# A planner that counts GpSimd's transfers on the common line of transfers, a release time for the accumulations of w_in, and batch 3 masked by TensorE

## The chip, the cores and the metric

The kernel runs on one core of a Trainium2 chip. Its time is the device time of one launch in microseconds (us); the time before is the median of three runs. The profile is of one further execution. The engines are named as in the profile: PE (TensorE, matrix products), DVE (VectorE), ACT (ScalarE), POOL (GpSimd) and SP (SyncE). SP does nothing but issue transfers; POOL issues those that add to what is already in SBUF.

## The reference

The program is an attention with two branches and, on its output, an MLP whose non-linearity is a rational function. Cut to what matters:

```
# q, k, v: 8 batches x 8 heads x 576 positions x 64
out_d     = softmax(mean4(q) @ mean4(k).T / 8) @ mean4(v)       # 144 pooled positions
out_up    = repeat(out_d, 4)
out_local = softmax(where(|i-j| < 4, q @ k.T / 8, -1e9)) @ v
x = (out_up + out_local)                                        # as 4608 tokens x 512
h = x @ w_in                                                    # 512 x 2048
P = a0 + a1 h + a2 h^2 + a3 h^3
Q = 1 + |b0||h| + |b1| h^2
out = (P / (Q + 1e-6)) @ w_out                                  # 2048 x 512
```

All inputs are float64 on the host's side, and w_in and w_out reach the chip as 64-bit words.

## The kernel before

**Blocks and steps.** The tokens are cut into nine blocks of 512: the first 512 tokens of each batch, and a last block of the eight leftovers of 64. A block takes 16 steps, one for each chunk of 128 of the 2048 hidden columns; 144 steps in all. Step n has a *first product* h(n) in PE (line 907 for the first sixteen steps, as plain fp32 with eight records in the profile each; from step 16 on line 919, with both factors split into a high and a low part and three of the four partial products), then the *rational function* (`middle`), and two steps later (`LAG = 2`) a *second product* into the output's banks (`o_part`, line 985, 12 matmuls of split parts). `middle` is six operations of ACT (all recorded at line 932: Abs, Square and two Identity from PSUM, which is what the names `m<-psum` and `gb<-psum` show; then Ln, `gb<-m`, and Exp, `m<-gb`) and seven of DVE (lines 947, 952 and 956, then 959, which writes the high part of g, 962, 967, and 968, which writes its low part).

**Weights.** They come in sixteen loads of 1 MB (`weights`; SP, line 356), each of two chunks of w_in or w_out, into six spots named sx0, sx1 and sl0 to sl3. sl2 and sl3 lie over attention tiles of batch 0. A load has to be turned from 64-bit words into fp32: ACT scales the upper words in place (line 363), DVE puts the parts together (366 and 369). w_out is then cast to its high part by ACT (399) and DVE takes the low part (402). w_in is used whole in the first sixteen steps, and split only after its use (`parts`): ACT writes the negative of the rounded word into the low part `wl` (line 424), POOL adds the exact word `wb` to it by an accumulating transfer (`accumulate`, line 411), and ACT then rounds the word in place to the high part `wh` (line 426).

**Attention.** `attend(b)` handles a batch in two halves of two pairs of heads. The pooled branch needs sums over four neighbours: `load_pooled` loads one of four slices by SP (line 466) and adds the other three by accumulating transfers of POOL (line 470), for two tiles pq (pooled q and k) and one tile vpc (pooled v). SP also loads qk (454) and vw (458) for the local branch. Batch 0 has its own code at the program's start. For the local scores there are two ways. In the batches that `PEMASK` lists, `scores` puts the mask into PSUM by four matmuls (line 491) ahead of the products, and `softmax_local` takes the maximum by DVE (line 534) and the exponentials by ACT (line 573) straight from PSUM. In the other batches `Half.scores` multiplies (line 700), DVE adds the mask on the way from PSUM to SBUF (line 713), and maximum (724) and exponentials (735) read SBUF.

**What sets the order.** No order is written by hand. Each operation is a task, added with its engine, a cost in us, what it reads and writes, and for some a due time (`Plan.add`). `Plan.run` first carries due times back from each task to its predecessors: the latest start of a task is that of its successor less its own cost and a lag (a fixed one by engine, or the task's own `lag`, 6.5 for an accumulation of w_in). It then plays the program forward on five engines: on each, of the tasks whose inputs are there, the one with the earliest latest start goes next (`HOLD` lets an engine wait a moment for a more urgent one). The instructions are then issued in the order of the planned starts. The plan sets only this order; on the chip an instruction waits for what it reads and for what stands ahead of it in its engine's queue. Two numbers set most due times: `due_h(n)`, the due time of step n's first product, is `H0` plus 6.11 for each of the first sixteen steps and 6.25 for each later one; a second product is due `O_LAG` steps behind that. Loads of the start have due times of their own (`LOADS`), which don't depend on H0; the due times of batch 0's attention do.

**Warm-up matmuls.** In planned idle time of PE at the start, `warm` (line 1124) puts dummy matmuls, up to the first task that is due at `due_h(0)`.

Of the kernel before, what the change touches and what calls it, by code (L numbers as in the profile page):

```python
# [14 lines left out]
ALU = mybir.AluOpType  # L15
# [9 lines left out]
POOL = 4  # L25
# [42 lines left out]


class Task:  # L70
    __slots__ = ("engine", "dur", "fn", "due", "preds", "succs", "late", "start", "end", "n", "lag", "uses")


class Plan:
# [8 lines left out]
        self.writer = {}  # L83
        self.readers = {}

    def add(self, engine, dur, fn, reads=(), writes=(), due=None, lag=None):
        t = Task()
        t.engine, t.dur, t.fn, t.due, t.n = engine, dur, fn, due, len(self.tasks)
        t.lag, t.preds, t.succs, t.late, t.start = lag, {}, [], 1e9, None
        rk = set().union(*(r.keys for r in reads)) if reads else set()  # L90
        wk = set().union(*(w.keys for w in writes)) if writes else set()
        t.uses = {k[1]: k in wk for k in rk | wk if k[0] == "P"}
        for k in rk | wk:
            w = self.writer.get(k)
            if w is not None:
                t.preds[w] = True
        for k in wk:
            for r in self.readers.get(k, ()):
                t.preds.setdefault(r, False)
            self.writer[k] = t  # L100
            self.readers[k] = []
        for k in rk - wk:
            self.readers[k].append(t) if k in self.readers else self.readers.__setitem__(k, [t])
        t.preds.pop(t, None)
        for p in t.preds:
            p.succs.append(t)
        self.tasks.append(t)
        return t
# [8 lines left out]
    def run(self):  # L117
# [8 lines left out]
        free = dict.fromkeys(self.LAG, 0.0)  # L126

        def release(t):
            at = 0.0
            for p in t.preds:  # L130
                at = max(at, p.end + self.gap(p, t))
            heapq.heappush(waiting[t.engine], (at, t.n, t))
# [5 lines left out]
        while len(done) < len(self.tasks):  # L138
            best = None
            for e in self.LAG:  # L140
                if open_[e]:
                    at = free[e]
# [26 lines left out]
                t = o[2]  # L169
            t.start, t.end = at, at + t.dur  # L170
            free[e] = t.end
            done.append(t)
            for s in t.succs:
                left[s] -= 1
# [9 lines left out]
def attention_moe(  # L184
# [162 lines left out]
    def weights(w, f, spot, due=None):  # L347
# [30 lines left out]
        if added:  # L378
            hi, lo = high2[w][f // 2], low2[w][f // 2]
            if f >= CAST:  # L380
                add(
                    "POOL", 1.0, lambda: nc.gpsimd.dma_start(out=flat2(hi), in_=flat2(word).bitcast(F32)),
                    (room,), (hi,), lag=CLAG,
                )
            else:
                add("ACT", 0.88, lambda: nc.scalar.copy(out=hi.ap, in_=word.ap.bitcast(F32)), (room,), (hi,))
# [21 lines left out]
    def accumulate(lo, word, room, due=None):  # L408
        add(
            "POOL", 1.0,  # L410
            lambda: nc.gpsimd.dma_start(out=flat2(lo), in_=flat2(word).bitcast(F32), accum_op=ALU.add),
            (room, lo), (lo,), due=due, lag=ALAG,
        )

    def parts(w, f, due=None):
# [44 lines left out]
    def load_pooled(cs):  # L460
# [4 lines left out]
        for dst, cost, src in loads:  # L465
            add("SP", cost, lambda d=dst, x=src[0]: nc.sync.dma_start(out=d.ap, in_=x), (), (dst,))
            for x in src[1:]:
                add(
                    "POOL", 1.0,
                    lambda d=dst, x=x: nc.gpsimd.dma_start(out=d.ap, in_=x, accum_op=ALU.add),  # L470
                    (dst,), (dst,), lag=4.0,
                )

    def pool_qk(c):
# [459 lines left out]
    def middle(n):  # L934
# [16 lines left out]
        )  # L951
        add("DVE", 0.61, lambda: v.tensor_tensor(out=ta.ap, in0=ta.ap, in1=tq.ap, op=ALU.mult), (ta, tq), (ta,))  # L952
        if UN[0] <= n < UN[1]:
            add("POOL", 0.95, lambda: nc.gpsimd.dma_start(out=ta.ap, in_=u.ap, accum_op=ALU.add), (ta, u), (ta,), lag=ULAG)
        else:
            add("DVE", 0.61, lambda: v.tensor_tensor(out=ta.ap, in0=ta.ap, in1=u.ap, op=ALU.add), (ta, u), (ta,))  # L956
        act(0.63, log, tb, tb.ap, AF.Ln, bias=cone)
# [82 lines left out]
    for r, x in enumerate(vf):  # L1040
# [1 line left out]
        add(  # L1042
            "POOL", 1.0,
            lambda r=r, x=x: nc.gpsimd.dma_start(out=x.ap, in_=vp[0, 2 + r], accum_op=ALU.add),
            (x,), (x,), lag=7.0,
        )
    early = LOADS[3]
    for (w, f, spot), due in zip(chunks[: len(early)], early):
# [109 lines left out]
NAT = 16  # L1158
HFIRST = (7, 5)
LAG = 2  # L1160
O_LAG = 2.11
H0 = 25.89
H_FIRST = 6.11
H_STEP = 6.25
SPLIT_EARLY = 9.53
# [8 lines left out]
DEFER = 1  # L1174
CAST = 99
CLAG = 6.0
NEG = 1
MINUS = (0, 1, 2, 3)
ADDED = (99, 99)
PEMASK = (1, 2)  # L1180


_OUTS = [((NT, DM), "float32")]
# [63 lines left out]
```

## Time and profile before

| | |
|---|---|
| median of 3 runs | 971.71 us (971.13 to 972.02) |
| the profiled execution | 968.8 us |
| its span in the trace | 966.9 us |
| granted PE clock, mean | 0.993 |
| PE busy | 943.1 us, 98% |
| DVE busy | 843.7 us, 87% |
| ACT busy | 813.4 us, 84% |
| POOL busy | 120.8 us, 12% |
| transfers by SP and hardware queues (q1) | 63.52 MB, 19.6% of 16 engines' span |
| transfers issued by POOL (q0) | 24.50 MB, 17.4% |

"Busy" counts the time in which an engine has an instruction under way, and an operation that waits inside for data may count as busy. The granted clock is 1.00 where PE may run at full rate. In a row of the timeline the first number is the start in us from the span's begin, the second the length, and a bracket behind it the idle time ahead of it on its engine with what ended that. Buffer numbers are left out there: sl stands for sl0 to sl3, wh for all high parts. A DMA row's time is that of its issue; when the data has landed is a separate number.

### The profile page before, as it was taken

How to read it: one execution, taken by the hardware profiler on the slowest of the kernel's cores; microseconds unless marked ns; L12 is line 12 of the kernel's file. 1: busy time of each engine (PE TensorE's matmuls, PEld its weight loads, DVE VectorE, ACT ScalarE, POOL GpSimd, SP SyncE). 2: the span in 40 equal slices, each digit the busy share in tenths (PEclk: the TensorE clock that was granted, in tenths of full speed). 3: DMA queues.
4: the chain of work that ended last, by engine and by line, in shares of the span. 5: the costliest groups of instructions: out<-in, count | busy, mean ns of one | idle time of the engine just before them, and what ended most of it. 6: DMA issues, size and time to landing. Idle time of an engine off the chain costs nothing.

```text
span 966.9 us, 19321 instructions
## 1 busy us (share of the span) xinstructions
PE 943.1 (98%) x7192; PEld 740.8 (77%) x7192; DVE 843.7 (87%) x1434; ACT 813.4 (84%) x1992; POOL 120.8 (12%) x144
## 2 busy tenths in 40 slices
PE   7879999999999999999999999999999999999996
PEld 5546657887888788787887787878878888888885
DVE  7779999898888989898889898898979899988885
ACT  3789999999789897979798979988797977778774
POOL 1212112021202020212111110212021000000000
PEclk9989999999999999999999999999999999999998
DMA  9995386344433433333333433334332010001001
GB/s 296 314 333 136 113 224 116 117 78 106 81 102 57 106 59 112 74 82 76 91 91 70 93 68 107 57 102 70 98 69 58 1 44 1 1 1 45 1 0 44
DMA packets 44318, 89.26 MB, mean 92 GB/s; under 512 B 4992, under 2 KB 25856, under 8 KB 44224
## 3 DMA queue, kind: packets, MB, share of 16 engines
q1 hardware_dynamic: 25344, 63.52, 19.6%
q0 software_dynamic: 18880, 24.50, 17.4%
q8 instruction: 57, 0.93, 0.4%
q14 instruction: 37, 0.30, 0.1%
HBM read 74.37 MB, written 9.44 MB: 87 GB/s over the span
## 4 chain that ended last, share of the span: by engine, by line
PE 59%; DVE 20%; ACT 14%; issue 4%; DMA 2%; DVEq 0%; POOL 0%; SPq 0%; ACTq 0%; POOLq 0%
PE psum L985 27%; PE psum L919 24%; ACT el L735 4%; ACT m L932 3%; DVE g L959 3%; DVE m L962 2%; DVE m L967 2%; PE psum L907 2%; ACT epc L599 2%; DVE m L956 2%; DVE g L968 2%; DMA sl<-in_w_in_dram 2%; ACT epc L616 2%; DVE m L952 1%; DVE m L947 1%
## 5 line engine op out<-in xcount | busy, mean ns | idle before, releaser
L985 PE MATMUL psum<-wh,g 128*128 128x512 f32 x1152 | 393.1, 402 | 7.8 <-DVE g L959 5.9
L932 ACT ACTIVATE m<-psum,cf 128x512 f32<-128x512 f32 x288 | 214.1, 748 | 60.1 <-PE psum L919 52.1
L985 PEld LDWEIGHTS psum<-wh,g 128*128 128x128 f32 x1152 | 214.4, 188 | 62.2 <-DVE g L959 9.6
L919 PE MATMUL psum<-xs,wh 128*128 128x512 f32 x1024 | 260.6, 394 | 0.0
L985 PE MATMUL psum<-wl,g 128*128 128x512 f32 x576 | 225.4, 392 | 0.0
L919 PEld LDWEIGHTS psum<-xs,wh 128*128 128x128 f32 x1024 | 189.5, 188 | 41.4 <-issue 1.2
L959 DVE TENSOR_TENSOR g<-m,m 128x512 fp32r<-128x512 f32 x144 | 99.4, 690 | 78.5 <-ACT m L932 73.0
L919 PE MATMUL psum<-xs,wl 128*128 128x512 f32 x512 | 137.5, 390 | 0.0
L985 PEld LDWEIGHTS psum<-wl,g 128*128 128x128 f32 x576 | 109.0, 189 | 23.2 <-issue 1.7
L932 ACT ACTIVATE gb<-psum,cf 128x512 f32<-128x512 f32 x144 | 115.7, 804 | 12.8 <-PE psum L985 12.8
L932 ACT ACTIVATE gb<-m,cf 128x512 f32<-128x512 f32 x144 | 107.4, 746 | 19.2 <-DVE m L947 14.8
L470 POOL DMA_DIRECT2D pq<-in_qkp_dram x84 | 73.7, 922 | 366.0 <-DMA pq<-in_qkp_dram 275.5
L919 PEld LDWEIGHTS psum<-xs,wl 128*128 128x128 f32 x512 | 95.9, 188 | 20.4 <-issue 0.2
L932 ACT ACTIVATE m<-gb 128x512 f32<-128x512 f32 x144 | 93.5, 649 | 20.7 <-DVE m L952 19.2
L947 DVE SCALAR_TENSOR_TENSOR m<-m,cf,m 128x512 f32<-128x512 f32 x144 | 107.3, 745 | 3.3 <-ACT m L932 3.2
L956 DVE TENSOR_TENSOR m<-m,gb 128x512 f32<-128x512 f32 x144 | 98.7, 685 | 6.5
L962 DVE SCALAR_TENSOR_TENSOR m<-m,g 128x512 f32<-128x512 f32 x144 | 99.2, 689 | 3.4
L968 DVE TENSOR_TENSOR g<-m,m 128x512 fp32r<-128x512 f32 x144 | 98.6, 685 | 3.3
L967 DVE TENSOR_TENSOR m<-m,m 128x512 f32<-128x512 f32 x144 | 99.0, 687 | 2.2
L952 DVE TENSOR_TENSOR m<-m,m 128x512 f32<-128x512 f32 x144 | 98.4, 683 | 0.0
L932 ACT ACTIVATE m<-psum 128x512 f32<-128x512 f32 x144 | 88.4, 614 | 0.0
L735 ACT ACTIVATE el<-el,nm 128x64 f32<-128x64 f32 x200 | 66.7, 336 | 1.4 <-DVE nm L729 0.7
(78 smaller groups left out, 920.3 us busy)
## 6 DMA issues: line engine op xcount, KB each, us to landing
qk<-in_qk_dram SPq DMA_DIRECT2D x32, 590.0 KB, 3.9
pq<-in_qkp_dram POOLq DMA_DIRECT2D x84, 144.0 KB, 3.3
vw<-in_vw_dram SPq DMA_DIRECT2D x32, 320.0 KB, 4.0
out_dram<-xf SPq DMA_DIRECT2D x32, 256.0 KB, 2.4
vpc<-in_vp_dram POOLq DMA_DIRECT2D x42, 168.0 KB, 3.5
sx<-in_w_in_dram SPq DMA_DIRECT2D x5, 1024.0 KB, 13.6
sl<-in_w_out_dram SPq DMA_DIRECT2D x4, 1024.0 KB, 16.7
sx<-in_w_out_dram SPq DMA_DIRECT2D x4, 1024.0 KB, 8.1
```

The source lines that it names most:

```text
L470: lambda d=dst, x=x: nc.gpsimd.dma_start(out=d.ap, in_=x, accum_op=ALU.add),
L735: nc.scalar.activation(out=e[:, n], in_=e[:, n], func=AF.Exp, bias=nm[:, n : n + 1], scale=scale, accum_out=sm[:, n : n + 1],)
L919: nc.tensor.matmul(ph.ap[:, f * t : (f + 1) * t], lhsT=(high, low)[j][0][fc].ap[:, c, :], rhs=blk.x[i].ap[:, c, :] if blk.b is not None el ...
L932: add("ACT", cost, lambda: nc.scalar.activation(out=out_.ap, in_=in_, func=func, **kw), (room_in, cf, *more), (out_,))
L947: lambda: v.scalar_tensor_tensor(out=tb.ap, in0=tq.ap, scalar=b1, in1=tb.ap, op0=ALU.mult, op1=ALU.add),
L952: add("DVE", 0.61, lambda: v.tensor_tensor(out=ta.ap, in0=ta.ap, in1=tq.ap, op=ALU.mult), (ta, tq), (ta,))
L956: add("DVE", 0.61, lambda: v.tensor_tensor(out=ta.ap, in0=ta.ap, in1=u.ap, op=ALU.add), (ta, u), (ta,))
L959: add("DVE", 0.61, lambda: v.tensor_tensor(out=gh.ap, in0=ta.ap, in1=tq.ap, op=ALU.mult), (ta, tq), (gh,))
L962: lambda: v.scalar_tensor_tensor(out=tb.ap, in0=tb.ap, scalar=CONE, in1=gh.ap.bitcast(F32), op0=ALU.add, op1=ALU.mult),
L967: add("DVE", 0.61, lambda: v.tensor_tensor(out=tb.ap, in0=ta.ap, in1=tb.ap, op=ALU.subtract), (ta, tb), (tb,))
L968: add("DVE", 0.61, lambda: v.tensor_tensor(out=gl.ap, in0=tb.ap, in1=tq.ap, op=ALU.mult), (tb, tq), (gl,))
L985: nc.tensor.matmul(ob[sub].ap, lhsT=g[i].ap[:, f0 : f0 + P], rhs=flat((high, low)[j][1][fc].ap), start=(fc == 0 and m == 0), stop=(fc == N ...
```

## The change

It has three parts, all in the planner's input; no operation of steps, weights or softmax is written differently.

1. *Transfers of POOL count on SP's line.* A task may carry a `load`. When such a task is planned, SP's line is busy from then on for that long (3.0 us for an accumulation of w_in, 0.8 for one of pq or vpc, 1.5 for one of vf), and the task's own lag becomes the time until that line is free again plus 2.2 us.
2. *The accumulations of w_in have a release time.* A task may carry an `after`, before which the plan does not start it; for an accumulation it is its due time plus 12.08 us. As the due time is 2 us ahead of the first split product of that chunk (step 16 and on), the plan's release lies behind step 16's first product.
3. *Constants.* `O_LAG` goes from 2.11 to 2.09, `H0` from 25.89 to 14.21, so that all due times of steps are 11.68 us earlier in the plan, and `PEMASK` takes in batch 3.

```diff
-    def add(self, engine, dur, fn, reads=(), writes=(), due=None, lag=None):
+    def add(self, engine, dur, fn, reads=(), writes=(), due=None, lag=None, load=0.0, after=0.0):
...
+        t.load, t.after = load, after
...
         def release(t):
-            at = 0.0
+            at = t.after
             for p in t.preds:
                 at = max(at, p.end + self.gap(p, t))
...
             t.start, t.end = at, at + t.dur
             free[e] = t.end
+            if t.load:
+                free["SP"] = max(free["SP"], t.end) + t.load
+                t.lag = free["SP"] - t.end + 2.2
...
     def accumulate(lo, word, room, due=None):
             lambda: nc.gpsimd.dma_start(out=flat2(lo), in_=flat2(word).bitcast(F32), accum_op=ALU.add),
-            (room, lo), (lo,), due=due, lag=ALAG,
+            (room, lo), (lo,), due=due, lag=ALAG, load=3.0, after=0.0 if due is None else due - DEFERRED,
...
     def load_pooled(cs):
-                    (dst,), (dst,), lag=4.0,
+                    (dst,), (dst,), lag=4.0, load=0.8,
...
-O_LAG = 2.11
-H0 = 25.89
+O_LAG = 2.09
+H0 = 14.21
+DEFERRED = -12.08
-PEMASK = (1, 2)
+PEMASK = (1, 2, 3)
```

Two further places that get a `load` (a cast by POOL and a sum inside `middle`) are switched off by other constants. In the changed kernel the lines of the body stand four further down: 363 is 367, 411 is 415, 932 is 936, 985 is 989.

The order of the instructions changes at the program's start, on ACT, POOL and SP, and there are 24 warm-up matmuls fewer on PE (32 instead of 56). ACT around step 0, whose first operations of the rational function are `m2_134<-psum` and `m4_136<-psum`; `sx0` is a spot of weights, `wl0_4` the low part of a chunk of w_in, `up` a part of batch 0's attention output. Before:

```order
L839 ACTIVATE up0_160<-psum 64x144
L839 ACTIVATE up1_161<-psum 64x144
L363 ACTIVATE sx0_189<-sx0_189 128x1024
L424 ACTIVATE wl0_4_58<-wb0_4_85 128x1024
L932 ACTIVATE m2_134<-psum,cf_150 128x512
L932 ACTIVATE m4_136<-psum 128x512
```

and now:

```order
L843 ACTIVATE up0_160<-psum 64x144
L843 ACTIVATE up1_161<-psum 64x144
L936 ACTIVATE m2_134<-psum,cf_150 128x512
L936 ACTIVATE m4_136<-psum 128x512
L936 ACTIVATE m0_132<-psum,cf_150 128x512
```

The scaling of sx0 and the copy into wl0_4 have left the place ahead of step 0; the scaling now stands behind step 3. Further on, ACT around step 1, whose last two operations of the six are Ln (`gb3_145<-m3_135`) and Exp (`m5_137<-gb3_145`). Before:

```order
L932 ACTIVATE m3_135<-psum,cf_150 128x512
L932 ACTIVATE m5_137<-psum 128x512
L363 ACTIVATE sl2_193<-sl2_193 128x1024
L363 ACTIVATE sl3_194<-sl3_194 128x1024
L932 ACTIVATE m0_132<-psum,cf_150 128x512
L932 ACTIVATE gb3_145<-m3_135,cf_150 128x512
L573 ACTIVATE el0_167,sm0_156<-psum,nm0_152 128x64 x5
```

and now:

```order
L936 ACTIVATE m3_135<-psum,cf_150 128x512
L936 ACTIVATE m5_137<-psum 128x512
L367 ACTIVATE sl2_193<-sl2_193 128x1024
L936 ACTIVATE m0_132<-psum,cf_150 128x512
L936 ACTIVATE gb3_145<-m3_135,cf_150 128x512
L936 ACTIVATE m2_134<-psum,cf_150 128x512
L577 ACTIVATE el0_167,sm0_156<-psum,nm0_152 128x64 x5
L936 ACTIVATE m5_137<-gb3_145 128x512
```

One scaling instead of two stands there now; that of sl3 has moved behind step 2's exponential.

The transfers that POOL issues, from batch 1's sums on (`wl0_0<-wb0_0` is the first accumulation of w_in). Before:

```order
L470 DMA pq0_165<-in_qkp_dram 128x288
L470 DMA pq1_170<-in_qkp_dram 128x288
L411 DMA wl0_0_56<-wb0_0_81 128x1024
L470 DMA pq0_165<-in_qkp_dram 128x288
L470 DMA pq1_170<-in_qkp_dram 128x288
L470 DMA vpc_174<-in_vp_dram 112x384
L411 DMA wl0_2_57<-wb0_2_83 128x1024
```

and now, the second half of batch 1 with what follows:

```order
L474 DMA pq0_165<-in_qkp_dram 128x288
L474 DMA pq1_170<-in_qkp_dram 128x288
L474 DMA vpc_174<-in_vp_dram 112x384 x3
L415 DMA wl0_0_56<-wb0_0_81 128x1024
L474 DMA pq0_165<-in_qkp_dram 128x288
L474 DMA pq1_170<-in_qkp_dram 128x288
```

All sums of both halves of batch 1 now come ahead of the first accumulation, where three accumulations stood between those of its first half; the second accumulation stands two rounds of batch 2's pq sums further on.

SP's order moves with them: sl2's load, once issued behind vpc, sx0, vw0 and vw1, now comes directly behind qk1 and ahead of those four; sl3's comes right behind vpc's. On ACT the two casts of line 426 for wh0_0 and wh0_2 now stand behind step 13's exponential. In batch 3 four pairs change from the rows of lines 713, 724 and 735 to those of 491, 534 and 573, and in batches 4 to 7 a handful of rows around their tenth and eleventh steps change places.

More of the change, by code (lines that the diff above doesn't have):

```diff
@@ L70 @@
 class Task:
-    __slots__ = ("engine", "dur", "fn", "due", "preds", "succs", "late", "start", "end", "n", "lag", "uses")
+    __slots__ = ("engine", "dur", "fn", "due", "preds", "succs", "late", "start", "end", "n", "lag", "uses", "load", "after")
 class Plan:
@@ L382, in weights @@
                     "POOL", 1.0, lambda: nc.gpsimd.dma_start(out=flat2(hi), in_=flat2(word).bitcast(F32)),
-                    (room,), (hi,), lag=CLAG,
+                    (room,), (hi,), lag=CLAG, load=3.0,
                 )
@@ L953, in middle @@
         if UN[0] <= n < UN[1]:
-            add("POOL", 0.95, lambda: nc.gpsimd.dma_start(out=ta.ap, in_=u.ap, accum_op=ALU.add), (ta, u), (ta,), lag=ULAG)
+            add("POOL", 0.95, lambda: nc.gpsimd.dma_start(out=ta.ap, in_=u.ap, accum_op=ALU.add), (ta, u), (ta,), lag=ULAG, load=1.5)
         else:
@@ L1044, in attention_moe @@
             lambda r=r, x=x: nc.gpsimd.dma_start(out=x.ap, in_=vp[0, 2 + r], accum_op=ALU.add),
-            (x,), (x,), lag=7.0,
+            (x,), (x,), lag=7.0, load=1.5,
         )
```

## The prediction

> **What bounds the kernel now.** I read first the busy times by stretch, then the chain that ended last where TensorE (PE) is idle, then the rows of ScalarE (ACT) and PE around that place. The page's first line and the stretches (columns: length, then PE, weight loads, VectorE (DVE), ACT and GpSimd (POOL) busy, granted PE clock, DMA share, GB/s):
>
> ```profile
> span 966.9 us, 19321 instructions
> 40.00:63.30 23.30, 16.65 (x93) 8.34 (x83) 13.94 (x25) 14.89 (x36) 7.02 (x8) 0.93 1.08 299
> 63.30:67.00 3.70, 3.70 (x49) 2.71 (x50) 3.20 (x6) 3.70 (x10) 0.00 (x0) 0.54 1.05 351
> 67.00:130.00 63.00, 63.00 (x434) 39.22 (x434) 61.61 (x104) 61.83 (x158) 9.87 (x11) 1.00 0.58 164
> 130.00:205.00 75.00, 74.51 (x511) 55.49 (x510) 70.74 (x122) 73.50 (x179) 14.91 (x17) 1.00 0.57 132
> 205.00:780.00 575.00, 573.36 (x4736) 462.61 (x4735) 503.26 (x890) 503.71 (x1346) 80.80 (x94) 1.00 0.36 79
> ```
>
> From 67 us on PE never rests for more than a few tenths; there only PE work counts. From 67 to 205 ACT and DVE are nearly as full (1.2 and 1.5 us, 1.4 and 4.3 us idle). Time is lost before that: in 40 to 63.3 PE is idle for 6.6 us while the DMA engines are full, and the clock drops. The chain there (start, us, what):
>
> ```profile
> 40.30 0.38 SPq L356
> 40.78 17.30 DMA sl<-in_w_in_dram
> 58.10 0.02 ACT sl L363
> 62.53 0.70 DVE g L959
> 63.28 2.06 PE psum L985 x4
> ```
>
> A weight chunk takes 17.3 us to land; ACT, which works in order, stands before its scaling (L363), and behind that scaling are the rational function's operations of step 1 that PE needs. The same on ACT and PE (brackets: idle before, and what ended it):
>
> ```profile
> 44.85 1.14 ACT L363 ACTIVATE sx<-sx 128x1024 f32<-128x1024 f32 x1 [4.44 <-DMA sx<-in_w_out_dram]
> 46.95 0.69 ACT L932 ACTIVATE m<-psum,cf 128x512 f32<-128x512 f32 x1
> 50.60 0.65 ACT L932 ACTIVATE m<-gb 128x512 f32<-128x512 f32 x1
> 58.10 1.13 ACT L363 ACTIVATE sl<-sl 128x1024 f32<-128x1024 f32 x1 [3.05 <-DMA sl<-in_w_in_dram]
> 61.85 0.65 ACT L932 ACTIVATE m<-gb 128x512 f32<-128x512 f32 x1
> ...
> 41.04 7.10 PE L907 MATMUL psum<-xf,wb 128*128 128x512 f32 x16 [0.89 <-DVE xf L666]
> 48.91 1.12 PE L907 MATMUL psum<-xf,wb 128*128 128x512 f32 x2
> 52.03 0.50 PE L985 MATMUL psum<-wh,g 128*128 128x512 f32 x1 [2.00 <-DVE g L959]
> 53.62 0.63 PE L985 MATMUL psum<-wl,g 128*128 128x512 f32 x1
> 54.05 0.63 PE L985 MATMUL psum<-wh,g 128*128 128x512 f32 x1
> 63.28 0.78 PE L985 MATMUL psum<-wh,g 128*128 128x512 f32 x1 [3.48 <-DVE g L959]
> 67.08 0.40 PE L985 MATMUL psum<-wl,g 128*128 128x512 f32 x1
> 67.31 0.39 PE L985 MATMUL psum<-wh,g 128*128 128x512 f32 x1
> ```
>
> Two stalls, 2.00 us before step 0's second product and 3.48 us before step 1's. After each PE runs at half rate for a while: 0.43 us from 53.62 to 54.05, against 0.23 us from 67.08 to 67.31. The clock column prices it: 7% of 23.3 us is 1.6, 46% of 3.7 us is 1.7. Gaps and half rate together are about 5.5 + 3.3 = 8.8 us.
>
> **The change, part by part.**
>
> *ACT's order at step 0.* Before, step 0's ten operations stand behind the scaling of sx0 (which waited 4.44 us) and a 1.0 us copy; now they come directly after the four `up` copies. They need step 0's first product. That ends with the fourth of the sixteen records from 41.04: each takes 7.10/16 = 0.44, so 42.8, and I put the first operation at 43.0 instead of 46.95. Step 0's exponential (m<-gb) begins 3.65 us later before (50.60 against 46.95), and PE's 52.03 is 1.43 behind that, so g is ready at 43.0 + 3.65 + 1.43 = 48.1. PE gets there at 48.91 + 1.12 = 50.0. The 2.00 us gap and its half-rate stretch go.
>
> *ACT's order at step 1.* Now one scaling (sl2) and not two stands before step 1's exponential, and sl3's moves behind step 2. From 43.0: ten L932 operations at 0.6 (six take the 3.65 above), 6.1; the scaling, 1.1; three more, 1.8; five exponentials of attention, 1.5; that is 53.5, and with about 1 us of waiting for DVE the exponential begins at 54 instead of 61.85. g is ready at 55.4. PE from 50.0 does twelve w_out products at 0.23 and six fp32 records at 0.44 first, 5.4 us: it comes at 55.4 as well. The 3.48 us gap and its half-rate stretch go. At step 1's second product the program is 63.28 − 55.4 = 7.9 us ahead, and 1.7 us more by 67: 9.6.
>
> *The transfers.* This needs sl2 to have landed by 49. The rows on that:
>
> ```profile
> DMA to landing us min/median/max: 13.6/15.4/17.3
> ...
> sx<-in_w_out_dram SPq DMA_DIRECT2D x1, 1024.0 KB, 4.9
> ...
> L411 POOL DMA_DIRECT2D wl<-wb x3: 1227/1257/1579, 32.5 to 51.8; - x3
> ...
> wl<-wb POOLq DMA_DIRECT2D x8, 512.0 KB, 10.9
> ```
>
> The first is the two sl loads issued at 40.3 and 40.8, the second the same size on a quiet queue at 94 us, the third the three accumulations that POOL issued between 32.5 and 51.8. In the new order all three stand behind both halves of batch 1, so 1.5 MB of read-and-add traffic leaves that stretch. SP's order changes too: sl2 now stands ahead of vpc, sx0 and vw, and cannot be issued before 40.3 (the chain's SP row is that issue; it overwrites tiles that batch 0 still reads). So SP waits from 30 to 40.3 with vpc, sx0 and both vw behind it. None of these four is used before 65 us; the price is that the DMA engines run dry for some 2 us before 40.3. In return sl2 is alone: between 4.9 (quiet) and 13.6 us (as before), landing between 45 and 54. I take 6, 46.5, nearest to the quiet row, since only pq accumulations are beside it. At 13.6 the step 1 term shrinks by 5.
>
> *What ACT and DVE give back.* PE can only keep the 9.6 us if ACT and DVE follow through 67 to 205. In 40 to 67 ACT is idle 27.0 − 14.9 − 3.7 = 8.4 us; of this it keeps about 2.6 (waiting for step 0's first product) and 1.0 (DVE), so 4.8 are won; with its 2.7 idle in 67 to 205 that allows 7.5. Counting the new ACT order, the work ahead of the exponentials of steps 5 to 21 is 0 to 3.4 us less than before. DVE: idle 27.0 − 13.9 − 3.2 = 9.9, keeps about 3, and 1.4 up to 130 allow 8.3. ACT's chunk for step 6 (sl3, now three places later) makes PE wait about 0.9 us around 73, and ACT's casts behind step 13 (the last rival) I give 0.6. So from 9.6: 7.5 by ACT's bound, less 1.5, so 6.0 us. Below, 4.8, if ACT finds no more idle time after 67 than now; above, 9.6 plus the 0.5 of idle time in 130 to 205.
>
> *Fewer warm-ups.* With the step due times 11.7 us earlier the filler stops sooner: two groups of twelve dummy matmuls vanish.
>
> ```profile
> 23.76 1.47 PE L1124 MATMUL psum<-ident,identb 128*128 128x256 bf16 x12
> 25.39 1.47 PE L1124 MATMUL psum<-ident,identb 128*128 128x256 bf16 x12
> 26.79 0.72 PE L815 MATMUL psum<-eptc,vf 48*64 48x144 f32 x16
> ```
>
> They filled waits, so they cost nothing before, and their going leaves PE idle for about 1.1 and 1.2 us, each shorter than the 2.00 us gap behind which half rate is seen. I take 0; if the clock falls here, 1.7 us as at 63.3, twice at most 3.4. [...]
>
> *Batch 3 masked by PE.* Four pairs change. Rows: a masked pair (from its first mask matmul to the next large one), an unmasked one, and DVE's mask addition.
>
> ```profile
> 165.23 0.33 PE L491 MATMUL psum<-maskb,identb 64*64 64x320 bf16 x4
> 166.07 1.45 PE L985 MATMUL psum<-wh,g 128*128 128x512 f32 x5
> 278.59 0.81 PE L700 MATMUL psum<-qk 64*64 64x64 f32 x40
> 279.33 1.20 PE L919 MATMUL psum<-xs,wh 128*128 128x512 f32 x4
> L713 DVE TENSOR_TENSOR el<-psum,maskd 128x640 f32<-128x640 f32 x20 | 16.3, 816 | 0.0
> ```
>
> 0.84 against 0.74: PE gains 0.10 of work a pair, +0.4 us. DVE loses 4 × 0.82 = 3.3 us of work off the path. In 205 to 780 PE waits 1.64 us in all; batch 3's part of that may go, 0.3. Net +0.1. The few rows that move in batches 4 to 7 shift one late product 1.8 us forward in PE and its inputs forward in ACT and DVE: 0, within ±1.6 (the present waits).
>
> The sum: 966.9 − 6.0 + 0.1 = 961.0 of span; the profiled execution's own time is 1.9 above its span, so 962.9. The median of the runs, 971.71, is 2.9 above the profiled 968.8; I carry that over: **965.8 us**.
>
> **The rivals.**
>
> *Absorbed.* ACT and DVE, or a slow sl2 (54), hold PE back: gain 2 to 4.8, 968.3. For: ACT's 98% in 67 to 205, and SP standing at sl2. Against: the accumulations' removal, and ACT's lighter list.
>
> *All of it.* The waits inside ACT's busy time shrink: −9.5, 962.2. For: much of what counts as busy in 67 to 205 is waiting for PE. Against: DVE's 61.61 of 63.
>
> *Cold clock.* The two idle spots halve the clock at 29 to 36 us, where the first fp32 products run: 1.7 to 3.4 back, 967.7.
>
> *It does not do what it says.* The new rule delays the accumulations only in the plan: no wait in the program holds them, so POOL issues the first as soon as batch 1's sums are through, near 100 us and not behind step 16. That alone costs nothing, as the DMA share is 0.58 there. If the weight loads then land no sooner, the waits just change their place: 971.7.
>
> *Slower.* ACT's casts of w_in's high parts (wh0_0, wh0_2) now stand right behind step 13's exponential, and each overwrites what an accumulation reads. The second accumulation stands on POOL behind two rounds of batch 2's pq sums. Those sums before, from the issue of what they add to, and step 13's second product:
>
> ```profile
> 127.94 1.25 SPq L466 DMA_DIRECT2D pq<-in_qkp_dram  x2
> ...
> 137.57 1.76 POOL L470 DMA_DIRECT2D pq<-in_qkp_dram  x2 [13.03 <-DMA pq<-in_qkp_dram]
> 144.45 1.75 POOL L470 DMA_DIRECT2D pq<-in_qkp_dram  x2 [5.12 <-DMA pq<-in_qkp_dram]
> ...
> 154.51 0.79 PE L985 MATMUL psum<-wh,g 128*128 128x512 f32 x1
> ```
>
> At that pace the second round ends near 151 and the accumulation lands 10.9 later, 162, while step 13's second product, which needs that exponential, began at 154.51. So ACT could stand there up to 7 us, with steps 14 to 16 behind it and PE after it. Each us beyond the need costs one; from 6.0 + 1.9 = 7.9 us on it ends slower, 974. For: the row. Against: two accumulations leave the queue just ahead of those sums, some 1 MB, so that the load lands earlier than 9 us after its issue.
>
> **How the numbers follow.** Forecast (963.5 to 967.0) 0.48; absorbed 0.21; all of it 0.12; cold clock 0.08; moved waits 0.05; slower 0.06. About 0.2% (1.9 us) is what a measurement of this kernel can tell from no change: faster means below 969.8. Faster: 0.48 + 0.12 and nearly all of absorbed and cold clock, 0.85; same 0.09; slower 0.06. The range reaches from all of it, 961.8, to the upper end of absorbed, 970.2.
>
> **What would show it.** Right: no gap over 0.5 us before the second products (L985, then L989) at 50 to 56, the granted clock at 1.00 from 40 to 70, step 1's second product at about 55.5, sl landing within 7 us, ACT over 97% busy from 60 to 195. Wrong: ACT standing at the scaling of sl2 or at a cast behind step 13; a clock of 0.5 near 30 us; or PE gaps in 60 to 200 that add up to more than 4 us.

## The result, and the profile after

The changed kernel takes **962.22 us** (median of 4 runs, 961.4 to 964.66) against 971.42 (4 runs, 969.15 to 972.02) of the kernel before: ratio **0.9914, 95% interval 0.9889 to 0.9938**. The profiled execution took 961.83 us, its span is 960.0 against 966.9.

The page's first line and the stretches of the kernel after (columns as before: length, PE, weight loads, DVE, ACT, POOL, granted clock, DMA share, GB/s):

```profile
span 960.0 us, 19318 instructions
40.00:63.30 23.30, 22.66 (x149) 12.78 (x150) 20.30 (x33) 20.23 (x64) 4.21 (x5) 1.00 1.03 340
63.30:67.00 3.70, 3.70 (x35) 2.46 (x34) 3.67 (x9) 3.70 (x7) 0.00 (x0) 1.00 0.68 138
67.00:130.00 63.00, 61.61 (x410) 37.54 (x408) 62.02 (x105) 61.68 (x153) 11.23 (x12) 1.00 0.63 174
130.00:205.00 75.00, 73.67 (x546) 56.42 (x546) 69.43 (x120) 73.62 (x172) 16.68 (x19) 1.00 0.62 133
205.00:780.00 575.00, 573.69 (x4718) 463.37 (x4717) 503.49 (x884) 501.14 (x1339) 80.96 (x94) 1.00 0.36 78
```

In 40 to 63.3 PE is idle for 0.6 us instead of 6.6, and the clock stays at 1.00 to 67 us. New in the table is that PE is idle for 1.4 us in 67 to 130, where it had none. The rows of ACT, PE and DVE at steps 0 to 2, and the landing of sl2 (the first of the last two rows is its issue):

```profile
42.95 0.69 ACT L936 ACTIVATE m<-psum,cf 128x512 f32<-128x512 f32 x1 [3.43 <-PE psum L911]
47.30 0.69 DVE L963 TENSOR_TENSOR g<-m,m 128x512 fp32r<-128x512 f32 x1 [0.98 <-ACT m L936]
48.85 1.18 ACT L367 ACTIVATE sl<-sl 128x1024 f32<-128x1024 f32 x1
53.45 0.66 ACT L936 ACTIVATE m<-gb 128x512 f32<-128x512 f32 x1
64.53 1.30 ACT L367 ACTIVATE sl<-sl 128x1024 f32<-128x1024 f32 x1
...
48.48 0.80 PE L989 MATMUL psum<-wh,g 128*128 128x512 f32 x1
54.99 0.50 PE L989 MATMUL psum<-wh,g 128*128 128x512 f32 x1 [0.60 <-DVE g L963]
61.93 0.79 PE L989 MATMUL psum<-wh,g 128*128 128x512 f32 x1
...
39.56 0.38 SPq L360 DMA_DIRECT2D sl<-in_w_out_dram  x1
DMA to landing us min/median/max: 6.8/6.8/6.8
```

Step 1's second product starts at 54.99 instead of 63.28 and has waited 0.60 us instead of 3.48. sl2 lands 6.8 us behind its issue, at 46.4, ahead of ACT's scaling at 48.85.

How far the change is ahead, read from the first record of line 985 (989 now) of each step:

| step's second product | before | after | ahead |
|---|---|---|---|
| 0 | 52.03 | 48.48 | 3.55 |
| 1 | 63.28 | 54.99 | 8.29 |
| 2 | 71.73 | 61.93 | 9.80 |
| 3 | 79.04 | 69.22 | 9.82 |
| 4 | 88.08 | 79.83 | 8.25 |
| 9 | 122.85 | 115.04 | 7.81 |
| 16 | 172.62 | 165.59 | 7.02 |
| 60 | 457.25 | 450.09 | 7.16 |
| last record | 958.86 | 951.82 | 7.04 |

So 9.8 us are won by step 2, 2.8 are given back between steps 3 and 16, and after that the lead only moves to and fro, between 6.3 and 7.5 us.

The table compares two single executions in absolute time, and part of each lead arises ahead of the steps. The second group of 16 matmuls of line 819 (815 before) starts when ACT has copied `eptc`, at 27.06 us against 28.13, so the change is 1.07 us ahead there already. Executions of kernels that share the change's start lie between 26.55 and 28.13 us at this place (last section), so up to about 1 us of every lead can be scatter. Counted from this place, called the wait at line 819 from here on, 8.7 us are won by step 2 and 6.0 remain at the end. The places in which PE waits in the change, where the kernel before had no wait:

```profile
74.15 2.81 PE L911 MATMUL psum<-xf,wb 128*128 128x512 f32 x6 [0.72 <-DVE wb L373]
79.27 1.12 PE L911 MATMUL psum<-xf,wb 128*128 128x512 f32 x2 [0.66 <-ACT gb L936]
131.88 0.53 PE L989 MATMUL psum<-wh,g 128*128 128x512 f32 x1 [0.66 <-DVE g L963]
151.68 1.20 PE L989 MATMUL psum<-wh,g 128*128 128x512 f32 x4 [0.49 <-DVE g L972]
```

The first waits for the words of sl3 (`wb`, joined by DVE), the second for ACT's operations. The last goes back to the first of the two casts behind step 13: ACT's cast of `xs` stands directly behind it, DVE waits 0.53 us for `xs`, and PE 0.49 us for DVE:

```profile
147.20 1.42 DVE L890 TENSOR_TENSOR xs<-xf,xs 128x512 fp32r<-128x512 f32 x2 [0.53 <-ACT xs L887]
```

The accumulations and the casts, on POOL and ACT:

```profile
98.25 0.96 POOL L415 DMA_DIRECT2D wl<-wb  x1
132.28 1.22 POOL L415 DMA_DIRECT2D wl<-wb  x1
...
145.08 1.05 ACT L430 CAST wh<-wb 128x1024 fp32r<-128x1024 f32 x1
147.68 1.05 ACT L430 CAST wh<-wb 128x1024 fp32r<-128x1024 f32 x1
```

On the chip the first accumulation is issued at 98 us, behind step 6 and not behind step 16; neither cast has idle time in front of it.

### The profile page after: what moved, and what is told of

Its sections match the earlier page's. It is cut to its first block, busy times and chain, and to the rows that moved or that the text cites. A ratio compares the mean times of both kernels' runs of the same rounds, so it can differ in the third digit from the quotient of the medians.

```text
span 960.0 us, 19318 instructions
## 1 busy us (share of the span) xinstructions
PE 939.1 (98%) x7184; PEld 738.1 (77%) x7184; DVE 843.4 (88%) x1430; ACT 812.4 (85%) x1992; POOL 121.1 (13%) x144
## 4 chain that ended last, share of the span: by engine, by line
PE 58%; ACT 20%; DVE 17%; issue 4%; DVEq 0%; POOL 0%; ACTq 0%; POOLq 0%
PE psum L989 26%; PE psum L923 25%; ACT m L936 6%; ACT el L739 4%; ACT epc L603 2%; DVE g L963 2%; DVE m L966 2%; DVE m L971 2%; ACT gb L936 2%; DVE g L972 2%; PE psum L911 2%; DVE m L951 1%; ACT epc L620 1%; DVE m L956 1%; DVE m L960 1%
## 5 line engine op out<-in xcount | busy, mean ns | idle before, releaser
L474 POOL DMA_DIRECT2D vpc<-in_vp_dram x42 | 34.9, 830 | 216.3 <-DMA vpc<-in_vp_dram 201.8
```

## The experiments

Beside each run's median and its ratio to the kernel before (that of the change is 0.9914, 0.9889 to 0.9938) two numbers of its trace are given: the start of step 1's second product, and the time from step 0's second product to that of the last step (904.08 us before, 900.57 in the change). The second is far sharper than a median: kernels with the same code up to some step agree in it to 0.05 us up to step 9 and to 0.2 us up to step 30, while medians of one kernel moved by a microsecond or two between sets of runs (before: 971.4, 970.3, 970.2, 970.2, 969.4). It leaves out what happens ahead of step 0, and that is part of the gain. Where it matters, the time from the wait at line 819 to the second product of the last step is given too: 927.98 us before, 921.99 in the change, 5.99 less.

### Which part of the change carries it

**The release time alone.** No counting, old due times, old mask:

```diff
-            if t.load:
+            if False:
...
-O_LAG = 2.09
-H0 = 14.21
+O_LAG = 2.11
+H0 = 25.89
-PEMASK = (1, 2, 3)
+PEMASK = (1, 2)
```

> The kernel before with the release time of the accumulations alone: POOL's transfers are not counted on SP's line, due times and mask as before. POOL issues no accumulation of w_in before batch 2's sums, so 1.5 MB of read-and-add traffic leaves 32 to 52 us; ACT's order around steps 0 and 1 stays as before (scaling of sx0 ahead of step 0, of sl2 and sl3 ahead of step 1's exponential), and sl2 stays behind vpc, sx0 and vw on SP. Theory A (ACT's order gives the gain): ACT still stands at the scaling of sx0 for 2 to 4 us and at sl3 for 1 to 3; step 1's second product starts at 59 to 62 instead of 63.28 before and 54.99 in the change; 966 to 970 us. Theory B (the traffic alone gives it): the loads land in time, step 1's second product near 55.5, 961.5 to 963.5.

Measured: 964.04 us, 0.9935 (0.9921 to 0.9948); step 1's second product at 57.36; 902.07. ACT's and PE's rows:

```profile
42.21 1.15 ACT L367 ACTIVATE sx<-sx 128x1024 f32<-128x1024 f32 x1 [1.99 <-DMA sx<-in_w_out_dram]
50.21 1.18 ACT L367 ACTIVATE sl<-sl 128x1024 f32<-128x1024 f32 x1
52.15 1.16 ACT L367 ACTIVATE sl<-sl 128x1024 f32<-128x1024 f32 x1 [0.76 <-DMA sl<-in_w_in_dram]
...
57.36 0.50 PE L989 MATMUL psum<-wh,g 128*128 128x512 f32 x1 [1.73 <-DVE g L963]
```

Neither theory as it was stated. ACT's order is that of before, and still the waits shrink: for sx0 from 4.44 to 1.99 us, for sl2 and sl3 from 0.89 and 3.05 to none and 0.76. With three accumulations gone from that stretch the loads land that much sooner. The loads of sl2 and sl3, first in the kernel before and then in this one:

```profile
DMA to landing us min/median/max: 13.6/15.4/17.3
DMA to landing us min/median/max: 8.0/9.8/11.5
```

That is 5.9 of the 8.3 us at step 1, 4.5 of the 6.0 us from the wait at line 819 to the end (923.50), and 0.65% of the 0.86% in the ratio, where each has its own runs of the kernel before.

**Without the counting** (release time, new due times and mask stay):

```diff
-            if t.load:
+            if False:
```

> The changed kernel without the counting of POOL's transfers: release time, new due times and mask stay. At the start ACT's and SP's order are those of before (sx0 ahead of step 0, sl2 and sl3 ahead of step 1's exponential). If the missing 2.4 us of lead at step 1 in the run with the release alone come from the order that the counting gives, this kernel is like that run: step 1's second product near 57.4 and 963.3 to 964.6 us. If they come from the due times or the mask, it is like the change: near 55 and 961.5 to 962.6.

Measured: 963.69 us, 0.9937 (0.9924 to 0.9950); 58.60; 902.10.

```profile
42.71 1.14 ACT L367 ACTIVATE sx<-sx 128x1024 f32<-128x1024 f32 x1 [2.04 <-DMA sx<-in_w_out_dram]
53.40 1.17 ACT L367 ACTIVATE sl<-sl 128x1024 f32<-128x1024 f32 x1 [1.52 <-DMA sl<-in_w_in_dram]
...
58.60 0.50 PE L989 MATMUL psum<-wh,g 128*128 128x512 f32 x1 [2.46 <-DVE g L963]
```

As in the run with the release alone, not as in the change: the same two waits of ACT are there, and the median lies in the range given for that. Step 1's second product comes 1.2 us later than there, 0.5 of it at step 0 already. So what the counting adds is the order at the start, worth 1.5 us from step 0 to the end (902.1 against 900.57) and 1.5 us in the medians.

**Without the release time** (counting, due times and mask stay):

```diff
-            at = t.after
+            at = 0.0
```

> The changed kernel without the release time: transfers counted, new due times, batch 3 masked by PE, but the first two accumulations of w_in stand first in POOL's queue, ahead of batch 1's sums, and sl1's scaling stands between steps 0 and 1 on ACT. Step 0's rational function still stands ahead of sx0's scaling. Theory A: step 0's second product is as early as in the change (48 to 49), but the accumulations delay sl1 and sl2 by some us, and ACT stands at their scaling: step 1's second product at 57 to 61, 964 to 968. Theory B: as the traffic is back, the waits of before are back: step 1's second product at 62 or later, 969 to 972.

Measured: 966.02 us, 0.9958 (0.9945 to 0.9972); 54.76; 903.96. The order at steps 0 and 1 gives the whole lead at step 1, with two accumulations ahead of batch 1's sums. One step later it is gone:

```profile
48.61 1.08 ACT L430 CAST wh<-wb 128x1024 fp32r<-128x1024 f32 x1
49.54 1.20 ACT L367 ACTIVATE sl<-sl 128x1024 f32<-128x1024 f32 x1
54.67 1.20 ACT L367 ACTIVATE sl<-sl 128x1024 f32<-128x1024 f32 x1
55.69 0.75 ACT L936 ACTIVATE m<-psum,cf 128x512 f32<-128x512 f32 x1
...
65.19 1.24 PE L522 MATMUL psum<-pq 64*64 64x144 f32 x17 [2.52 <-ACT m L936]
```

A cast and two scalings stand between steps 0 and 2 on ACT, step 2's first operation starts at 55.69 instead of 51.43, and PE waits 2.52 us; step 2's second product starts at 67.76 instead of 61.93. That these three come there follows from the accumulations' early place in the plan. The end lies 3.4 us behind the change, counted from step 0. The median lies in theory A's range, but not by theory A's way, and neither theory had this: the price of the early accumulations was expected at step 1, by way of late loads, and it came at step 2, by way of ACT's queue.

**The old due times** (counting, release and mask stay):

```diff
-O_LAG = 2.09
-H0 = 14.21
+O_LAG = 2.11
+H0 = 25.89
```

> The changed kernel with the old H0 and O_LAG: counting, release and mask stay. At the start ACT, SP and POOL keep the change's order up to step 3, the 56 warm-up matmuls are back, and the casts of w_in stand one to three places later. Theory A: the due times are no source of the gain: within 1 us of the change, 961 to 963.5, and step 1's second product at 54 to 55.5. Theory C (the due times, which are 11.7 us earlier, give most of it): 966 or more. If the clock's fall at 28 us in the change costs time, this kernel, which has the warm-ups, starts step 0 up to 1.5 us earlier.

Measured: 962.82 us, 0.9927 (0.9915 to 0.9940); 56.09, which is 6.51 us behind step 0's as in the change (6.51); 901.27. Theory A: from the start of the steps on, the due times are no source of the gain. The absolute 56.09 missed the stated 54 to 55.5 only because step 0 started 1.1 us later, not up to 1.5 earlier. Behind step 0 this kernel takes 0.7 us more, around step 16, where the casts stand later:

```profile
175.55 1.20 PE L923 MATMUL psum<-xs,wh 128*128 128x512 f32 x4 [0.89 <-ACT wh L430]
```

From the wait at line 819 it takes 922.12 us, 0.1 more than the change. Ahead of that place the due times may count for more. They move two loads of a mask (`maskd`) on SP from 14.33 us in the kernel before, ahead of the pq loads, to 18.86 us in the change, behind them. The three executions with the old due times reach the place at 27.97 to 28.73 us, the eleven with the new ones at 26.55 to 28.13. No run moved these loads alone, so whether they bring about 1 us is open.

**Batch 3's mask undone** (`PEMASK = (1, 2)` in the change).

> The changed kernel with batch 3 masked by DVE again. Theory A: the mask's place is worth next to nothing, as PE sets the time there: 961.9 to 962.6 against 962.2, ratio to before within 0.001 of the change's 0.9914. Rival: DVE's 3.3 us of mask additions in batch 3 cost time (or the four mask matmuls a pair do): over 963.2, or under 961.2; then the lead over the kernel before changes between steps 18 and 32, where batch 3's attention lies.

Measured: 962.74 us, 0.9927 (0.9915 to 0.9939); 900.96. Its profiled execution started step 0 1.08 us late and was still 0.95 behind the change at step 20, so nothing was lost up to there; at step 60 it is 1.36 behind. Batch 3's attention does not lie at steps 18 to 32, as the expectation has it, but at steps 32 to 41 (272 to 325 us in this run), while the loss arises behind that, 0.46 us at step 53 alone. So it is open whether even the 0.4 us of the trace belong to the mask's place. The median and the ratio lie just outside of what theory A allowed (by 0.1 us and 0.0003) and short of the rival's; they cannot tell it.

### The clock at 28 us

The 24 warm-up matmuls put back at their old places:

```diff
-    pe = [t for t in todo if t.engine == "PE" and t.start < due_h(0) + 5.0]
+    pe = [t for t in todo if t.engine == "PE" and t.start < 31.0]
...
-        if t.due is not None and t.due == due_h(0):
+        if t.start > 26.0 and t.due is not None and t.due >= due_h(0):
             break
```

> The changed kernel with the 24 dropped warm-up matmuls put back at their old places, nothing else. In the change PE stands idle for 2.15 us up to 27.06 and the granted clock is 0.90 in 20 to 30 and 0.93 in 30 to 40, one window at half rate, 1.7 us. Theory A (that window lies on the path to step 0): the clock is 1.00 there, step 0's first product starts 0.8 to 1.7 us earlier, and as ACT and DVE bound the stretch behind it some of this is lost: 960.8 to 962 against 962.2. Theory D (it is hidden behind ACT and DVE at 39 to 43 us): no difference, 961.9 to 962.5, and step 1's second product at 55.0.

Measured: 961.81 us, 0.9914 (0.9900 to 0.9927); 54.73; 900.58. The median lies in theory A's range and 0.1 us below theory D's; the trace decides for theory D, as step 0's first product starts only 0.3 us earlier, by as much as the wait at line 819. The stretch from 20 to 40 us and PE's waits, first the change, then this kernel:

```profile
20.00:40.00 20.00, 16.82 (x312) 13.06 (x310) 16.98 (x36) 15.68 (x42) 3.55 (x4) 0.91 0.90 282
27.06 1.39 PE L819 MATMUL psum<-eptc,vf 48*64 48x144 f32 x32 [2.15 <-ACT eptc L796]
40.04 7.10 PE L911 MATMUL psum<-xf,wb 128*128 128x512 f32 x16 [0.62 <-DVE xf L670]
```

```profile
20.00:40.00 20.00, 17.35 (x336) 13.81 (x334) 16.98 (x37) 15.44 (x42) 3.03 (x4) 1.00 0.86 276
26.80 1.21 PE L819 MATMUL psum<-eptc,vf 48*64 48x144 f32 x32 [0.63 <-ACT eptc L796]
32.36 1.10 PE L911 MATMUL psum<-xf,wb 128*128 128x512 f32 x2 [1.40 <-ACT et L796]
```

The clock does fall in the change, 9% of 20 us, one stretch at half rate (0.50 in 28 to 31 us), and it costs nothing: with the full clock PE waits 1.40 us for ACT's copies at 32.36 instead. From the wait at 27.06 (26.80) to step 0's second product both take 21.42 us. It is not always so cheap: the profiled execution of the run `dve_extra` below, whose code is the same up to step 6, shows 0.81 and 0.85 in 20 to 30 and 30 to 40, twice as much, and took 22.30 us for the same way, 0.9 more. If all of what is missing was at half rate, the granted clock of 20 to 40 us (0.91 and 0.83) makes, by estimate, about 3.6 and 6.8 us at half rate in these two executions. The wait at line 819 is as long in both (2.15 us in the change, 2.14 in `dve_extra`), so its length does not tell them apart; what does was not shown.

### What gives 2.8 us back between steps 3 and 16

One operation more, or fewer, on ACT or DVE, with all other instructions in their old order.

**More.** Steps 6 to 9, on ACT `nc.scalar.copy(out=log.ap, in_=log.ap)` behind the exponential; on DVE a second `tensor_tensor(out=tb.ap, in0=tb.ap, in1=tq.ap, op=ALU.mult)` behind line 972.

> The changed kernel with one more operation on ACT behind the exponential of steps 6, 7, 8 and 9 each (a copy of 128x512 in place, about 0.6 us, read by nobody), with nothing else moved: 2.4 us. If ACT and DVE bound the stretch from 67 to 205 us, as the prediction's sum took it, PE falls behind by about as much: 963.8 to 964.6. If PE itself bounds steps 5 to 16 and ACT's full busy time holds waits for PE, less than 0.6 us is lost: 962.0 to 962.8.

> The changed kernel with one more multiplication on DVE (128x512, 0.69 us, read by nobody) behind the last operation of steps 6, 7, 8 and 9 each, with nothing else moved: 2.8 us. If DVE bounds the stretch (62.02 us busy of 63 from 67 to 130), PE falls behind by 1.5 to 2.8 us: 963.7 to 965. If PE bounds it, less than 0.6: 962.0 to 962.8.

Measured: on ACT 963.66 us, 0.9935 (0.9920 to 0.9950), 902.52; on DVE 966.50 us, 0.9961 (0.9950 to 0.9971), 904.23. Against the change's 900.57 that is 1.95 us for 2.5 of work on ACT, and 3.66 us for 2.8 on DVE. The medians miss the ranges given for ACT and DVE, the first by 0.1 us below, the second by 1.5 above, and lie above those for PE. So neither engine has slack to give, and the theory that PE alone bounds this stretch is out. On DVE the delay is larger than the work; how much of that is later waits was not separated. The largest of them:

```profile
156.35 0.98 PE L997 MATMUL psum<-wh,g 128*128 128x512 f32 x3 [1.67 <-DVE g L980]
```

**Fewer.** Steps 3 to 6: on ACT no Ln, on DVE neither line 966 nor 971.

```diff
-        act(0.63, log, tb, tb.ap, AF.Ln, bias=cone)
-        act(0.54, tq, log, log.ap, AF.Exp, scale=-1.0)
+        if 3 <= n < 7:
+            add("ACT", 0.63, lambda: None, (tb, cf), (log,))
+            add("ACT", 0.54, lambda: nc.scalar.activation(out=tq.ap, in_=tb.ap, func=AF.Exp, scale=-1.0), (log, tb, cf), (tq,))
```

> The changed kernel with ACT's Ln of steps 3 to 6 left out (the exponential reads Ln's input instead), everything else in its old order: 4 x 0.75 us less on ACT, and that much less between the last input and the exponential of these steps; the output is no longer the reference's. In the change the lead over the kernel before falls from 9.8 us at step 3 to 7.8 at step 9. If ACT's work there takes it back, the lead stays above 9 and the kernel gains 1 to 2 us: 960.2 to 961.2. If DVE or the missing weight chunk (sl3, joined by DVE) takes it, less than 0.6: 961.6 to 962.5.

> The changed kernel with two of DVE's seven operations (0.69 us each, both on the way to g's low part only) left out in steps 3 to 6, everything else in its old order: 5.5 us less on DVE; g's low part, and so the output, is no longer the reference's. If DVE's work takes back the lead between steps 3 and 9, the join of sl3 and all behind it come earlier, the wait of 0.72 us at 74 us goes, the lead stays above 9 and the kernel gains 1 to 2 us: 960.2 to 961.2. If ACT takes it back, less than 0.6: 961.6 to 962.5.

Measured: ACT 961.58 us, 0.9914 (0.9899 to 0.9929), 899.74; DVE 962.30 us, 0.9920 (0.9905 to 0.9936), 900.79. The first median misses its range by 0.4 us and by its size is next to the other theory's; the trace tells them apart: without the Ln the kernel is 9.31 ahead of the one before at step 4 instead of 8.25, 7.95 at step 16 instead of 7.02, and ends 0.83 earlier. Without 5.5 us of DVE's work nothing is won (8.27 at step 4). PE's waits there, without the Ln, and without DVE's operations:

```profile
74.02 2.81 PE L911 MATMUL psum<-xf,wb 128*128 128x512 f32 x6 [0.55 <-DVE wb L373]
```

```profile
73.83 2.82 PE L911 MATMUL psum<-xf,wb 128*128 128x512 f32 x6 [0.39 <-ACT gb L936]
79.25 1.13 PE L911 MATMUL psum<-xf,wb 128*128 128x512 f32 x2 [0.96 <-ACT gb L936]
```

With less on DVE, PE waits for ACT at both places; with less on ACT the second wait is gone. At step 4 ACT decides, but only there: of the 3 us taken off it 1.09 are won by step 4 and nothing more by step 9. From 80 to 131 us PE is busy for 50.95 of 51 us in the change, so less work on ACT wins nothing there. DVE (50.40) and ACT (49.68) are nearly as full: an operation more on either costs time, one fewer wins next to none. Less work on both at once was not run.

**What is given back.** The traces of before and after show it, by ACT's busy time from the span's start to the start of a step's exponential (us):

| up to the exponential of step | before: time, ACT busy | after: time, ACT busy | idle time saved | work put off |
|---|---|---|---|---|
| 2 | 69.98, 43.56 | 59.17, 38.89 | 6.14 | 4.67 |
| 9 | 118.92, 91.52 | 111.44, 89.84 | 5.80 | 1.68 |
| 20 | 194.06, 165.16 | 187.11, 164.25 | 6.04 | 0.91 |

The idle time that ACT saves stays at about 6 us, 0.6 of it ahead of 40 us. What shrinks is work that the new order put off, such as the scalings of sx0 and sl3, and that comes due between steps 3 and 20.

**The join of sl3 earlier**, in the kernel with the warm-ups kept:

```diff
-        add("DVE", 1.13, lower, (spot, room), (room,))
+        add("DVE", 1.13, lower, (spot, room), (room,), due=due_h(f) - 6.0 if (w, f) == (0, 6) else None)
```

> The kernel with the warm-ups kept (961.81) with the joining of sl3's words (the DVE operation that PE waits for at 73.9 us) due 6 us earlier, which puts it seven places earlier on DVE. If the order of that join costs the 1.6 us of lead at step 4, the wait of 0.74 us goes, the lead at step 4 is 9.3 or more instead of 8.5, and the kernel comes out at 960.3 to 961.2. If ACT and DVE are simply full there, another operation is late in its place and the time stays: 961.5 to 962.3.

Measured: 962.25 us, 0.9918 (0.9904 to 0.9932); 900.63 against 900.58. The wait for the join is gone, and others stand in its place:

```profile
72.92 1.17 PE L989 MATMUL psum<-wh,g 128*128 128x512 f32 x4 [0.45 <-DVE g L972]
74.61 1.13 PE L911 MATMUL psum<-xf,wb 128*128 128x512 f32 x2 [0.52 <-ACT gb L936]
```

So the late chunk was only the operation that happened to be last.

**A version that might have been better**: batch 1's pooled weights divided on DVE instead of ACT, `EP_DVE = (0, 1)`, with the warm-ups kept.

> A version that may beat both: the kernel with the warm-ups kept (961.81) in which batch 1's pooled weights are divided by their sums on DVE (one operation a pair) instead of on ACT (three a pair, two groups of 1.22 us at 69.8 and 71.9 in the change). 4 pairs, so about 4.5 us leave ACT and 3 us come to DVE between 66 and 140 us, and the plan reorders the rest around it. Theory: leaving out ACT's Ln in steps 3 to 6 kept 1.06 us of lead at step 4, leaving out DVE's operations none, so ACT is the tighter one there: from step 0 to the end 0.5 to 1.2 us less than the 900.6 of the kernel with the warm-ups, 960.6 to 961.3. Rival: one more operation on DVE per step in steps 6 to 9 cost more (3.7 us for 2.8) than one on ACT (2.0 for 2.4), so what comes to DVE behind step 5 takes it back: 962 to 964.

Measured: 966.19 us, 0.9965 (0.9952 to 0.9977); 905.80. The rival held, and by more than it said: 1.6 us were lost at step 4 already (1.74 us of PE waiting for sl3's join on DVE) and 6.8 by step 16. In 67 to 130 ACT's busy time falls to 58.87 us and PE's with it:

```profile
67.00:130.00 63.00, 60.57 (x405) 36.77 (x404) 61.22 (x103) 58.87 (x141) 10.23 (x12) 1.00 0.61 174
```

What leaves ACT for DVE meets an engine that is as full (in 67 to 130 of the change DVE is busy for 62.02 of 63 us, ACT for 61.68). The loss is larger than the work moved; the plan also reordered the rest, and the two were not separated. No run beat the change clearly; the kernel with the warm-ups kept is its equal, and its clock does not fall (1.00 in 20 to 40 us).

## Why the prediction was right, and where it was off

The direction, the place and the range were right: 962.22 lies in 961.8 to 970.2, 1.3 us below the *Forecast's* own 963.5 to 967.0, and at the time that was given to *All of it* (962.2), though not by that rival's mechanism; that the two agree is chance. The range held with 0.4 us to spare, and its ends are not quite what the rivals give: *All of it* gives 962.2 and not 961.8, and a gain of 2 us 969.7 and not 970.2. 965.8 was 3.6 us too much: 1.1 from the sum and 2.5 from the last line.

- **Step 0 and step 1.** By its steps: ACT's first operation at 43.0 (42.95), g ready at 48.1 (47.30 + 0.69 = 48.0), sl2 landed at 46.5 (46.4), step 1's exponential at 54 (53.45), its second product at 55.4 (54.99), ahead by 9.6 with the clock (9.8). PE came to step 0's second product earlier than reckoned, 48.48 instead of 50.0; 1.07 of that is the earlier start at the wait at line 819. Of the signs, the gap ahead of step 1's second product was 0.60 for at most 0.5.
- **Why it works.** The prediction put the gain down to ACT's order, with the transfers as its condition. The runs weigh it the other way: the release time alone, with ACT's old order, gives 0.65% of 0.86%; the order that the counting makes adds 1.5 us; without the release that order holds for one step only, and 0.42% are left. The two do not add up, 0.65 and 0.42 being more than 0.86: part of the waits goes with either. The due times add 0.1 us from the wait at line 819 (0.7 from step 0), and for the mask's place no gain clear of the scatter is shown.
- **What ACT and DVE give back.** The term "from 9.6: 7.5 by ACT's bound, less 1.5, so 6.0" came out as 7.0 in absolute time, and as 6.0 (from 8.7) counted from the wait at line 819. So the 1.1 us by which the sum was off may be no more than the early start of one execution. What the term is made of came out otherwise. The bound counted on ACT's 2.7 us of idle time in 67 to 205 being won; ACT is as idle there as before (2.7 us, 135.30 busy of 138 against 135.33). In 40 to 67 ACT won 5.3 us for 4.8, and the rest of the lead is work put off. That 7.5 comes near the 7.8 us of step 9 is in part luck. Of the 1.5 taken off behind it, the 0.9 for sl3 "around 73" was counted twice: moving that wait away changed nothing (900.63 us from step 0 against 900.58), since ACT and DVE are full there (61.68 and 62.02 us busy of 63 in 67 to 130). The casts behind step 13 were put at 0.6, and a wait of 0.49 us goes back to them; from step 9 to step 16 0.8 us go in all (7.81 to 7.02), and what ends the wait of 0.66 us at 131.88 was not tested.
- **From the profiled execution to the median.** "The median of the runs, 971.71, is 2.9 above the profiled 968.8; I carry that over" failed: the changed kernel's profiled 961.83 is 0.4 below its median. Later runs of the kernel before lay between 967.9 and 972.4, so that its profiled execution was at the low end of a scatter, and this has no reason to recur.
- **The rivals.** *Absorbed* fell: the lead at the end is 7.0, or 6.0 from the wait at line 819, not 2 to 4.8. *All of it*: no, 2.8 of 9.8 were given back. *Cold clock* came, and with it one of the signs of being wrong, the clock of 0.5 near 30 us: the two gaps forecast at 1.1 and 1.2 us came as one of 2.15, longer than the 2.00 us behind which half rate was seen in the kernel before. It cost nothing; its price was taken from a place where PE's work counted, and here ACT's copies set the time (PE waits 1.40 us for them where the clock stays at 1.00). *It does not do what it says*: the half of it that was fact is so, the first accumulation goes out at 98 us, as forecast "near 100"; but the loads did land sooner. *Slower*: the second accumulation went out at 132.28, not behind 151, because batch 2's sums ran earlier and faster (126.78 to 131.74 us, where those before began at 137.57), and ACT did not stand at the casts.

## What to carry to other kernels

When a stretch is full of transfers, look first at what moves there without being needed there: taking 1.5 MB out of it gave more (964.04 us) than the new order with that traffic left in (966.02 us). A lead that an order wins by putting work off is partly given back when that work comes due; what stays is the idle time saved, so compare busy time up to the same operation in both traces. The operation that then shows as the last wait is part of that and not a further cost. An operation added to an engine tells whether it has slack, one taken away whether it alone is the limit; here the two answers differed. Where runs scatter by more than the effect, compare traces from a common point of the program on, and say which: the due times count for 0.1 or 0.7 us here, by the point chosen.

## What was not expected of the hardware

The scatter between runs arises ahead of step 0. Six profiled executions share the change's start (the change, `mask_undone`, and the four with more or less work on ACT or DVE). In these step 0's second product starts between 47.98 and 49.88 us; from there to step 1's all six take 6.51 or 6.52 us, and to step 3's 20.74 to 20.78. Two sources were seen. The wait at line 819 ends between 26.55 and 28.13 us, and about there the granted clock falls: its mean in 20 to 40 us is 0.91 to 0.92 in the change, `act_extra` and `mask_undone`, and 0.83 in `dve_extra`. `dve_extra` takes 22.30 us from there to step 0's second product, the other five take 21.42 or 21.43, 0.9 less. The first source is seen earlier already, in PE's scores at line 505 (15.51 us in `act_extra`, 16.01 in the change, 17.09 in `mask_undone`), among the program's first loads; what shifts it stays open.

A late start of this kind is not made up: `mask_undone` is 1.08 us behind the change at step 0 and 0.95 at step 20. A delay between steps 0 and 3 is in part: the kernel without the counting is 3.7 us behind the change at step 3 and 1.3 at step 60, both counted from step 0. That is the lead of the change over it shrinking, as the lead over the kernel before does.
